# Linear attention and a token-mixing layer on one core: values copied straight into chunk order, one token order for all tensors, full-height transposes

## The chip, the cores and the metric

The kernel runs on one core of a Trainium2 chip. The core has five engines, each with its own queue of instructions that it works off in order: TensorE (matrix multiplications; PE in the profile, with PEld for its weight loads), VectorE (DVE), ScalarE (ACT), GpSimd (POOL) and SyncE (SP), which here only issues DMA transfers. Engines wait for each other by semaphores. SBUF is the working memory with 128 partitions, PSUM the small memory of 8 banks into which TensorE writes.

The metric is the time of one execution on the device in microseconds (us), lower is better. Every kernel is run several times, and the median counts.

## What is computed

The first part is a linear attention with decay. For every batch and head a 48 x 48 state is carried over 768 tokens; its output is the input of the second part, in which every batch mixes its tokens through two learned projections.

```python
# r, k, v, w: (4 batches, 8 heads, 768 tokens, 48), float32; u: (8, 48)
for t in range(S):
    cur = np.einsum('bhd,bhe->bhde', u[None] * kt, vt)
    y[:, :, t] = np.einsum('bhd,bhde->bhe', rt, state + cur)
    state = wt[:, :, :, None] * state + np.einsum('bhd,bhe->bhde', kt, vt)
x = y.transpose(0, 2, 1, 3).reshape(B, S, 384)
wq, wk = x @ w_q, x @ w_k                      # 384 x 64 each
W_tok = (1 / 8) * np.einsum('bsd,btd->bst', wq, wk)
mixed = np.einsum('bst,btd->bsd', W_tok, x)
out = np.maximum(mixed, 0.0) @ w_out           # 384 x 384
```

## The kernel before

**Tiling.** The 768 tokens of a batch are three *units* of 256 tokens, so there are 12 units (n = 0 to 11; unit n belongs to batch n // 3). A unit holds two chunks (c = 0, 1) of 128 tokens. Heads are taken in four pairs (hp). In a loaded tile a partition holds neighbouring tokens: two for `load` (128 partitions, pieces of 2 x 48 floats = 384 bytes in HBM), four for `load_long` (64 places per chunk, pieces of 768 bytes; used for k and r of all units but the first). So the tokens of a chunk stand in an order of their own, and every step that turns a tile has to put them back.

**A unit's steps**, by the names under which the plan adds them:

- `wg kg rg vg`: loads of the four tensors, on SP's queue, into rings of four buffers each. `ln` (ScalarE): logarithm of the decay. `k16`, `r16` (GpSimd or ScalarE): casts to bf16.
- `cw` (TensorE): the sum of the logarithms along the tokens, as a product with the triangular matrix CM, for each chunk with the 64 rows that hold its tokens. `en`, `ep` (ScalarE): exponentials of minus and plus that sum; `ep` is two instructions, since it also changes the order.
- `kT`, `rT` (TensorE): transposes of k and r by the permutation PM, 16 matmuls of 64 rows each. `ks`: copy of the transposed k to SBUF. `qT = r * k`, `RT = r * ep` (VectorE), `KT = k * en` (GpSimd from `ks`, or VectorE from PSUM).
- Values: `v16` (GpSimd) casts to bf16, `vp` (TensorE) permutes the tokens by PM in four matmuls, `VB` (ScalarE) copies from PSUM. For the last batch v is loaded in pieces of 192 bytes by four transfers (`vw`, `load_whole`) straight into chunk order, and `VB` is one cast on GpSimd.
- `dps`, `dd`, `Vd`: the bonus u. `A` (TensorE): the 128 x 128 scores of every head; `AM` (VectorE): their mask. `kb`, `kd`, `sn`, `SB`: the new state. `yi`, `ya`, (`yv`): the output in PSUM; `X`: its copy to SBUF, on VectorE with the bonus added.
- `xt`, `XT`, `qk`, `QK`: transposes of X and the two projections.

When a batch's three units are done: `T`, `TS` (the mixing matrix), and for each of its units `mx` (product with it), `rl` (relu), `fp` (projection by w_out, 6 matmuls of 384 columns), `os` (copy to SBUF), `st` (store). The first and the last unit are cut into halves by chunk.

**What sets the order.** All steps are added to a `Plan`. ORDER is a permutation of them, written out: every engine gets its steps in just this order, whatever unit they belong to. WAYS gives the engine of each step that has a choice (A ScalarE, D VectorE, P GpSimd; E, e and c are forms of TensorE's steps, with e and c on parts of the array; N leaves a step out, T cuts the weights' load in two). BANKS gives the PSUM bank of each buffer. `yv` is there only where `X` is on ScalarE. All matmuls go through the helper `mm`, so that they share one line of the profile, and most copies share those of `copy`.

Of the kernel before, what the change touches and what calls it, by code (L numbers as in the profile page):

```python
# [10 lines left out]
F32 = mybir.dt.float32  # L11
# [21 lines left out]
class Plan:  # L33
# [85 lines left out]
]  # L119
WAYS = (  # L120
    "PPDPPDPPDDDDDDPDTTPDDAAPPDPPPADDDEENDEAAPPDdPADEAEENDEAAAPAPPADEDcNDEDAAAAAAAAPADdPAAEAc"
    "cNDEADPPDdPAAeAcENDeDAPPDPPAAeAENDEAAAAAAAAAPPDPPAAEDEENDEAAPPDdPAAeAEENDEAAPPDPPAAEAcND"
    "EDAAADAAAAPPDPPAEAEcNDeAAPPDPPAeAccNDeDAPPDPPPAPPAENDEDADNDEAADDDDAAAAAADDADNNEEEENEEENE"
    "NENENNNNNNEN"
)
BANKS = [
# [7 lines left out]
]  # L134


WARM = 24


@with_exitstack  # L140
def kernel(
# [27 lines left out]
    LONG = tuple(range(1, N))  # L169
    WHOLE = (B - 1,)  # L170

# [13 lines left out]
    def const(shape, dtype, name):  # L185
# [9 lines left out]
        wg=(4, HW, F32), rg=(4, HW, F32), kg=(4, HW, F32), vg=(4, HW, F32), os=(4, 2 * DM, F32),  # L195
        kd=(2, KW, BF16), lw=(2, 1024, BF16), r16=(2, 1024, BF16), k16=(2, 1024, BF16),
        ep=(2, 8 * EW, BF16), en=(2, 1024, BF16), ks=(2, 1024, BF16), qT=(2, 1024, BF16),
        RT=(2, 1024, BF16), KT=(2, 1024, BF16), v16=(2, 2 * DM, BF16), VB=(2, 2 * DM, BF16),
        dd=(2, 2 * H, F32), Vd=(2, 2 * DM, BF16), AM0=(2, 1024, BF16), AM1=(2, 1024, BF16),
        SB=(4, NP * D, BF16), XT=(2, 2 * DM, BF16), MX=(4, 2 * DM, BF16), X=(2, NCH * DM, BF16),  # L200
        QK=(2, QW, BF16), TS=(2, DM, BF16), vw=(2, NCH * DM, F32))
    if not WHOLE:
        del RINGS["vw"]
# [14 lines left out]
    PM = const([C, C], BF16, "PM")  # L218
# [3 lines left out]
    CM = const([C, 2 * C], BF16, "CM")  # L222
# [7 lines left out]

    def load_long(b, i, tl, ap, e):
        nc.sync.dma_start(  # L232
            out=view(tl, 0, [[2 * D2, NP], [1, 2 * D2]]),
            in_=dataclasses.replace(ap, offset=(b * H * S + i * U) * D,
                                    ap=[[4 * D, 64], [S * D, H], [1, 4 * D]]))

    def load_whole(b, q, tl):
        nc.sync.dma_start(
            out=view(tl, 0, [[D, H * NCH], [1, D]], p0=64 * (q % 2) + 32 * (q // 2), pn=32),
            in_=dataclasses.replace(v, offset=(b * H * S + q) * D,  # L240
                                    ap=[[4 * D, 32], [C * D, H * NCH], [1, D]]))
# [54 lines left out]
    def setup():  # L296
# [11 lines left out]
        runs = [[64, 2], [32, 2], [1, 32]]  # L308
# [5 lines left out]
        clear("C", CM, 1.0, cols=128)  # L314
        for c in range(2):
            for j in range(2):
                select("C%d%d" % (c, j), ["C"], view(CM, j * C, runs, p0=c * 64, pn=64), 128,
                       ALU.is_ge, pattern=[[1, 2], [2, 2], [4, 32]], base=-j,
                       channel_multiplier=-2)
# [3 lines left out]
        clear("P", PM, cols=64)  # L323
        select("PM", ["P"], view(PM, 0, runs), 128, ALU.not_equal, 1.0,
               pattern=[[64, 2], [1, 2], [2, 32]], base=0, channel_multiplier=-1)
# [6 lines left out]
        for q in range(4):  # L332
            select("U%d" % q, ["U"], view(US, 0, runs, p0=64 * (q % 2) + 32 * (q // 2), pn=32), 128,
                   ALU.is_gt, pattern=[[1, 2], [2, 2], [4, 32]], base=-q, channel_multiplier=-4)
# [5 lines left out]
    def dma(key, fn, after=(), buf=None, reads=()):  # L340
        return add(key, "ST" if key[0] in ("wts", "wo") else "S", fn, after, buf, reads)

    def weights():
# [16 lines left out]
        def cast(e):  # L360
            nc.gpsimd.tensor_scalar_mul(view(wq_sb, 0, [[128, NK], [64, 2], [1, DH]]),
                                        view(wq_f, 0, [[DH, NK], [0, 2], [1, DH]]), scale)
            nc.gpsimd.tensor_copy(view(wk_sb, 0, [[DH, NK], [32, 2], [1, 32]]),
                                  view(wk_f, 0, [[DH, NK], [1, 2], [2, 32]]))
# [14 lines left out]
    def unit(n, batch):  # L379
# [6 lines left out]
        whole, long = b in WHOLE, n in LONG  # L386
# [3 lines left out]
        for name, ap in (("wg", w), ("kg", k), ("rg", r)) + (() if whole else (("vg", v),)):  # L390
            f = load_long if name in ("kg", "rg") and long else load
            g[name] = ring(name)
            g[name + "L"] = dma((name, n), lambda e, ap=ap, f=f, x=g[name].tile: f(b, i, x, ap, e),
                                buf=g[name])
# [204 lines left out]
        for cs in ([(0,)] if final else fine):  # L599
# [13 lines left out]
            def f_kd(e, cs=cs):  # L613
                n4 = NP * len(cs)
                x = view(at(kb, BF16), cs[0] * NP * D, [[D, n4], [1024, 2], [1, D]])
                if kb.kind == "s":
                    x = view(at(kb, BF16), 0, [[C, n4], [64, 2], [1, D]])
# [288 lines left out]
```

## Time and profile before

| | |
|---|---|
| median of 3 runs | 103.31 us |
| the runs | 101.56, 103.31, 103.33 us |
| span of the profiled execution, first to last instruction | 101.1 us |
| its own time, with what lies around the span | not given apart from the runs; 0.5 to 2.2 us over the span, by the fastest run and the median |
| granted TensorE clock | 1.00 of full speed |
| busy: TensorE / VectorE / ScalarE / GpSimd | 86.8 / 80.5 / 80.9 / 68.8 us |
| read from and written to HBM | 19.66 MB, 4.72 MB |
| DMA packets | 45165, of which 31576 under 512 bytes |

Busy time is the time in which an engine had an instruction running; neighbouring instructions overlap a little, so the durations of a group add up to more than its busy time. "Idle before" is the time in which an engine waited just ahead of an instruction, and the arrow names what ended it. A matmul's duration has a fixed part (0.16 to 0.2 us) that overlaps with its neighbours; what a step costs TensorE is read from one step's start to the next one's.

### The profile page before, as it was taken

The numbers are of one execution on the slowest core, as the hardware profiler recorded it, in microseconds if no ns is written. First come the engines' busy times: TensorE is split into PE (matmuls) and PEld (weight loads), VectorE is DVE, ScalarE is ACT, GpSimd is POOL, SyncE is SP. The second block draws the span as 40 slices with busy tenths as digits, with TensorE's granted clock in tenths as the row PEclk, the third lists the DMA queues.
The fourth block names the chain that finished last, engine by engine and source line by source line (L and its number), as shares of the span: only waits on it lengthen the run. The fifth ranks groups of instructions, "written<-read, shape, count | busy, mean of one in ns | idle before, by whom it ended". The sixth has DMA issues, their size and how long they took to land.

```text
span 101.1 us, 4474 instructions
## 1 busy us (share of the span) xinstructions
PE 86.8 (86%) x1906; PEld 63.4 (63%) x1909; DVE 80.5 (80%) x134; ACT 80.9 (80%) x134; POOL 68.8 (68%) x82
## 2 busy tenths in 40 slices
PE   5966984989899888999899988999999998999920
PEld 1334553777597556678577875787877667776500
DVE  5423896899999989889999899999997897565520
ACT  5068975999799699599998999989997995735930
POOL 6858964699937764968899749999995897000000
PEclk9999999999999999999999999999999999999999
DMA  1999998999999999999999799999888831007591
GB/s 26 309 324 346 332 317 227 341 261 274 313 306 240 257 205 244 291 329 341 224 323 287 192 343 301 166 155 250 229 233 310 314 141 67 0 0 303 209 366 69
DMA packets 45165, 24.68 MB, mean 244 GB/s; under 512 B 31576, under 2 KB 43992, under 8 KB 45144
## 3 DMA queue, kind: packets, MB, share of 16 engines
q1 hardware_dynamic: 44984, 24.19, 86.9%
q8 instruction: 15, 0.25, 1.0%
q10 hardware_dynamic: 160, 0.20, 0.6%
q14 instruction: 6, 0.05, 0.2%
HBM read 19.66 MB, written 4.72 MB: 241 GB/s over the span
## 4 chain that ended last, share of the span: by engine, by line
PE 34%; ACT 15%; DMA 13%; DVE 12%; SPq 10%; issue 7%; POOL 4%; DVEq 0%; POOLq 0%; ACTq 0%
PE PS L177 34%; DMA vg<-in_v_dram 7%; DMA kg<-in_k_dram 6%; ACT ep L444 6%; SPq L227 5%; ACT en L451 4%; SPq L232 4%; DVE AM L592 3%; DVE X L724 2%; ACT os L275 2%; POOL v L281 2%; DVE ks L281 1%; POOL r L414 1%; DVE RT L513 1%; DVE qT L503 1%
## 5 line engine op out<-in xcount | busy, mean ns | idle before, releaser
L592 DVE TENSOR_TENSOR AM<-PS,US 128x1024 bf16<-128x1024 f32 x24 | 28.7, 1216 | 0.9 <-PE PS L177 0.6
L523 POOL TENSOR_TENSOR KT<-ks,en 128x1024 bf16<-128x1024 bf16 (+1 forms) x10 | 17.4, 1739 | 2.7 <-DVE qT L503 2.0
L572 POOL TENSOR_TENSOR Vd<-VB,dd 128x768 bf16<-128x768 bf16 (+1 forms) x14 | 18.0, 1292 | 1.5 <-ACT dd L275 1.0
L444 ACT ACTIVATE ep<-PS,kp 128x512 bf16<-128x512 f32 (+1 forms) x28 | 16.3, 646 | 0.1
L451 ACT ACTIVATE en<-PS,km 128x1024 bf16<-128x1024 f32 (+1 forms) x14 | 13.9, 1002 | 1.1 <-ACT QK L275 0.8
L724 DVE TENSOR_TENSOR X<-PS,Vd 128x768 bf16<-128x768 f32 (+1 forms) x13 | 11.6, 889 | 2.7 <-POOL Vd L572 1.4
L177 PE MATMUL PS<-wo,MX 128*128 128x384 bf16 x72 | 13.3, 326 | 0.2 <-ACT ep L444 0.2
L177 PEld LDWEIGHTS <-KT 48*128 48x128 bf16 (+1 forms) x312 | 10.3, 94 | 5.1 <-issue 2.6
L177 PE MATMUL PS<-RT,KT 48*128 48x128 bf16 x192 | 9.6, 217 | 1.9 <-POOL KT L523 1.0
L414 POOL CAST k<-kg 128x768 bf16<-128x768 f32 x10 | 8.2, 824 | 3.6 <-DMA kg<-in_k_dram 1.8
L281 DVE COPY ks<-PS 128x1024 bf16<-128x1024 bf16 x11 | 7.6, 689 | 3.7 <-PE PS L177 3.7
L275 ACT COPY os<-PS 128x768 f32<-128x768 f32 (+1 forms) x13 | 8.8, 679 | 1.9 <-PE PS L177 1.6
L414 POOL CAST r<-rg 128x768 bf16<-128x768 f32 x10 | 8.2, 824 | 3.1 <-DMA rg<-in_r_dram 1.9
L513 DVE TENSOR_TENSOR RT<-PS,ep 128x1024 bf16<-128x1024 bf16 (+1 forms) x14 | 8.5, 608 | 2.2 <-ACT ep L444 2.0
L403 ACT ACTIVATE lw<-wg 128x768 bf16<-128x768 f32 x12 | 10.1, 850 | 0.1
L177 PEld LDWEIGHTS <-MX 128*128 128x128 bf16 x72 | 6.4, 97 | 4.3 <-DVE MX L289 0.3
L287 ACT ACTIVATE MX<-PS 128x768 bf16<-128x768 f32 (+1 forms) x11 | 8.2, 758 | 0.9 <-PE PS L177 0.8
L275 ACT CAST VB<-PS 128x768 bf16<-128x768 f32 x9 | 7.3, 806 | 1.8 <-PE PS L177 1.7
L281 POOL CAST v<-vg 128x768 bf16<-128x768 f32 x9 | 7.4, 823 | 1.8 <-DMA vg<-in_v_dram 1.7
L177 PE MATMUL PS<-CM,lw 64*128 64x128 bf16 x192 | 7.9, 217 | 0.7 <-issue 0.4
L656 DVE TENSOR_TENSOR SB<-PS,ep 128x192 bf16<-128x192 f32 x20 | 7.0, 350 | 1.6 <-PE PS L177 1.5
L503 DVE TENSOR_TENSOR qT<-PS,ks 128x1024 bf16<-128x1024 bf16 x12 | 8.2, 681 | 0.0
(82 smaller groups left out, 182.8 us busy)
## 6 DMA issues: line engine op xcount, KB each, us to landing
kg<-in_k_dram SPq DMA_DIRECT2D x12, 384.0 KB, 5.5
wg<-in_w_dram SPq DMA_DIRECT2D x12, 384.0 KB, 6.3
rg<-in_r_dram SPq DMA_DIRECT2D x12, 384.0 KB, 6.4
vg<-in_v_dram SPq DMA_DIRECT2D x9, 384.0 KB, 6.9
out_dram<-os SPq DMA_DIRECT2D x9, 384.0 KB, 3.2
vw<-in_v_dram SPq DMA_DIRECT2D x4, 288.0 KB
out_dram<-os SPq DMA_DIRECT2D x5, 192.0 KB, 2.8
wof<-in_moe_w_out_dram SPq DMA_DIRECT2D x1, 450.0 KB
```

The source lines that it names most:

```text
L177: return nc.tensor.matmul(o, l, rr, start=start, stop=stop, skip_group_check=True, is_transpose=trans)
L275: nc.scalar.copy(o, i)
L281: x.tensor_copy(o, i)
L403: nc.scalar.activation(view(lw.tile, 0, [[64, H], [512, 2], [1, D]]), view(g["wg"].tile, 0, [[D2, H], [D, 2], [1, D]]), ACT.Ln, bias=0.0, ...
L414: op(view(o.tile, 0, [[64, NP], [256, 4], [1, D]]), view(g[src].tile, 0, [[2 * D2, NP], [D, 4], [1, D]]))
L444: nc.scalar.activation(view(ep.tile, cs[0] * NP * EW + off, [[EW, NP * len(cs)], [step, 2], [1, 32]]), view(at(cw), cs[0] * 512 + j * 64, ...
L451: nc.scalar.activation(en.tile[:, ds(cs[0] * 512, w_)], at(cw)[:, ds(cs[0] * 512, w_)], ACT.Exp, bias=km, scale=-1.0)
L513: nc.vector.tensor_tensor(plain(RT.tile, cs, 32), turned(512, cs, True), plain(ep.tile, cs, EW // 4), ALU.mult)
L523: x.tensor_tensor(KT.tile[:, cols], ks.tile[:, cols], en.tile[:, cols], ALU.mult)
L572: (nc.vector if e == "D" else nc.gpsimd).tensor_tensor(Vd.tile[:, cols], VB.tile[:, cols], view(dd.tile, cs[0] * H, [[1, len(cs) * H], [0, ...
L592: AMs[c] = add(("AM", n, c), "D", lambda e, c=c, A=A: nc.vector.tensor_tensor(view(AM[c].tile, 0, [[C, 8], [1, C]]), view(at(A), 0, [[C, 8 ...
L724: nc.vector.tensor_tensor(o, y_, view(Vd.tile, c0 * DM, dims), ALU.add)
```

## The change

- **One token order.** All tensors are loaded by `load`, two tokens to a partition, in pieces of 384 bytes; `load_long` and `load_whole` go. Within a chunk the order is now 64 odd tokens, then 64 even ones, for r, k, v, w, the mask US and the sums; the copies `QK` and the weights' cast no longer reorder.
- **Values.** `v16`, `vp`, `VB` go. `vu` and `vs` copy from the loaded tile into VB, each as two instructions of 64 partitions x 384 elements, float32 to bf16. `vu` stays on its partitions, `vs` moves between the lower and the upper half. `vs` is on VectorE (`VSW = "D"`); `vu` has a choice.
- **Transposes and sums.** `kT` and `rT` use all 128 rows and the identity, 8 matmuls of 128 columns; they have a PSUM bank each. `cw` is 8 matmuls of 256 columns over all 128 rows, with a matrix CM of double width in which the other chunk's rows are zero. PM goes.
- **One decay exponential.** `ep` is one instruction instead of two.
- **Smaller ones.** The weights are loaded in one part each. The ring `os` has 10 buffers instead of 4.
- **ORDER, WAYS and BANKS are new throughout.** Steps by engine:

| step | before | after |
|---|---|---|
| k16, r16 | GpSimd 22, ScalarE 2 | GpSimd 21, ScalarE 3 |
| values | v16 GpSimd 9, vp TensorE 9, VB ScalarE 9 and GpSimd 3 | vu GpSimd 11 and ScalarE 1, vs VectorE 12 (two instructions each) |
| ks | ScalarE 1, VectorE 11 | ScalarE 7, VectorE 5 |
| KT | GpSimd 10, VectorE 4 | GpSimd 9, VectorE 5 |
| X | VectorE 13 | VectorE 9, ScalarE 4 (with 4 yv on TensorE) |
| XT | ScalarE 8, VectorE 5 | ScalarE 9, VectorE 4 |
| os | ScalarE 13, VectorE 2 | ScalarE 7, VectorE 8 |
| dd | ScalarE 9, VectorE 3 | ScalarE 6, VectorE 6 |
| uC (start) | ScalarE | VectorE |

On SP's queue all loads come first, then all stores; before, one store stood between the loads of units 10 and 11. The first loads are w, k, r of unit 0 (before: k, w, w of unit 1, r). On TensorE all 15 `fp` steps come after `cw` of unit 11; before, the three of batch 0 stood ahead of `cw` of unit 9. The first `KT` is on VectorE.

```diff
-    def load_long(b, i, tl, ap, e):
...
-    def load_whole(b, q, tl):
...
 def f_cw(e):
     for hp in range(NP):
         for j in range(2):
-            for c in range(2):
-                mm(x[:, ds(c * 512 + hp * C, C)],
-                   lw.tile[ds(c * 64, 64), ds(j * 512 + hp * 128, 128)],
-                   CM[ds(c * 64, 64), ds(j * C, C)],
-                   start=(hp == 0 and j == 0), stop=(j == 1))
+            mm(x[:, ds(hp * U, U)], lw.tile[:, ds(j * 512 + hp * 128, 128)],
+               CM[:, ds(j * U, U)], start=(hp % 2 == 0 and j == 0), stop=(j == 1))
...
-            def f_ep(e, cs=cs, w_=w_):
-                for off, step, j in ((68, 34, 0), (34, -33, 1)):
-                    nc.scalar.activation(
...
+            def f_ep(e, cs=cs, many=many, step_=step_):
+                nc.scalar.activation(
+                    view(ep.tile, cs[0] * EW + 1, [[step_ * EW, many], [1, C]]),
+                    view(at(cw), cs[0] * C, [[step_ * C, many], [1, C]]), ACT.Exp, bias=kp,
+                    scale=1.0)
...
+        kt, rt = bank(), bank()
+        def transposed(name, src, step, o):
+            def f(e):
+                x = at(o, BF16)
                 for hp in range(NP):
                     for j in range(2):
+                        mm(view(x, hp * U + (1 - j) * 64, [[C, 2], [1, 64]]),
+                           src.tile[:, ds(j * 512 + hp * 128, 128)], ID16, trans=True)
...
+        def f_V(moved):
+            def f(e):
+                op = dict(A=nc.scalar.copy, D=nc.vector.tensor_copy, P=nc.gpsimd.tensor_copy)[e]
+                for c in range(2):
+                    half = (c + moved) % 2
+                    op(view(VB.tile, c * DM, [[1, DM]], p0=half * 64, pn=64),
+                       view(g["vg"].tile, (1 - half) * D, [[D2, H], [1, D]], p0=c * 64, pn=64))
+            return f
+        VBs = [add(("vu", n), "PAD", f_V(0), [g["vgL"]], VB, [g["vg"]])]
+        VBs.append(add(("vs", n), VSW, f_V(1), [g["vgL"]], VB, [g["vg"]]))
```

More of the change, by code (lines that the diff above doesn't have):

```diff
@@ L167 @@
     N = B * NU
-    LONG = tuple(range(1, N))
-    WHOLE = (B - 1,)
     SHIFT = 25
@@ L331, in setup @@
         clear("U", US, 1.0, cols=64)
-        for q in range(4):
-            select("U%d" % q, ["U"], view(US, 0, runs, p0=64 * (q % 2) + 32 * (q // 2), pn=32), 128,
-                   ALU.is_gt, pattern=[[1, 2], [2, 2], [4, 32]], base=-q, channel_multiplier=-4)
+        for c in range(2):
+            select("U%d" % c, ["U"], view(US, 0, runs, p0=c * 64, pn=64), 128, ALU.is_ge,
+                   pattern=[[-c, 2], [1, 64]], base=c - 1, channel_multiplier=-1)
         su["IU"] = add(("IU",), "DP", lambda e: on(e).tensor_scalar_mul(IDU, ID16, UNIT),
@@ L340, in dma @@
     def dma(key, fn, after=(), buf=None, reads=()):
-        return add(key, "ST" if key[0] in ("wts", "wo") else "S", fn, after, buf, reads)
+        return add(key, "S", fn, after, buf, reads)
     def weights():
@@ L385, in unit @@
         fine = each if split else both
-        whole, long = b in WHOLE, n in LONG
         new = (lambda *k: [su[x + str(n)] for x in k]) if n < 2 else lambda *k: []
         g = {}
-        for name, ap in (("wg", w), ("kg", k), ("rg", r)) + (() if whole else (("vg", v),)):
-            f = load_long if name in ("kg", "rg") and long else load
+        for name, ap in (("wg", w), ("kg", k), ("rg", r), ("vg", v)):
             g[name] = ring(name)
-            g[name + "L"] = dma((name, n), lambda e, ap=ap, f=f, x=g[name].tile: f(b, i, x, ap, e),
+            g[name + "L"] = dma((name, n), lambda e, ap=ap, x=g[name].tile: load(b, i, x, ap, e),
                                 buf=g[name])
-        if whole and i == 0:
-            batch["vw"] = ring("vw")
-            batch["vwL"] = [dma(("vw", n, q), lambda e, q=q, x=batch["vw"].tile:
-                                load_whole(b, q, x), buf=batch["vw"]) for q in range(4)]
         lw = ring("lw")
@@ L428, in f_cw @@
                 for j in range(2):
-                    for c in range(2):
-                        mm(x[:, ds(c * 512 + hp * C, C)],
-                           lw.tile[ds(c * 64, 64), ds(j * 512 + hp * 128, 128)],
-                           CM[ds(c * 64, 64), ds(j * C, C)],
-                           start=(hp == 0 and j == 0), stop=(j == 1))
-        cws = add(("cw", n), "E", f_cw, [ln] + [su["C%d%d" % x] for x in ((0, 0), (0, 1), (1, 0), (1, 1))] +
-                  new("lw"), cw, [lw], mode=1)
+                    mm(x[:, ds(hp * U, U)], lw.tile[:, ds(j * 512 + hp * 128, 128)],
+                       CM[:, ds(j * U, U)], start=(hp % 2 == 0 and j == 0), stop=(j == 1))
+        cws = add(("cw", n), "E", f_cw, [ln] + [su[x] for x in ("C00", "C01", "C10", "C11", "Z0", "Z1")] +
+                  new("lw"), cw, [lw])
         en, ep = ring("en"), ring("ep")
@@ L459, in unit @@
                 eps[c], ens[c] = x, y
-        kr = wide()
-        def transposed(name, src, step, place):
+        kt, rt = bank(), bank()
+        def transposed(name, src, step, o):
             def f(e):
-                o = at(kr, BF16)
-                if long:
-                    for hp in range(2):
-                        for s in range(4):
-                            for c in range(2):
-                                rows = ds(c * 64, 64)
-                                x = c * 1024 + place + hp * C + (s % 2) * 64 + (s // 2) * 32
-                                mm(view(o, x, [[256, 2], [1, 32]]),
-                                   src.tile[rows, ds(s * 256 + hp * 128, 128)],
-                                   PM[rows, rows], trans=True)
-                    return
+                x = at(o, BF16)
@@ L476, in f @@
                 for hp in range(NP):
                     for j in range(2):
-                        for c in range(2):
-                            rows = ds(c * 64, 64)
-                            mm(o[:, ds(c * 1024 + place + hp * C + j * 64, 64)],
-                               src.tile[rows, ds(j * 512 + hp * 128, 128)],
-                               PM[rows, rows], trans=True)
-            return add((name, n), "E", f, [step, su["PM"]] + new(name[0] + "16"), kr, [src], mode=1)
-        def turned(place, cs=(0, 1), runs=False):
-            return view(at(kr, BF16), place + cs[0] * 1024, [[1024, len(cs)]] * (len(cs) > 1) +
-                        ([[32, 16], [1, 32]] if runs else [[1, 512]]))
@@ L490, in plain @@
-        def plain(t, cs=(0, 1), run=0):
-            y = 16 * (run or 32)
-            return view(t, cs[0] * y, [[y, len(cs)]] * (len(cs) > 1) +
-                        ([[run, 16], [1, 32]] if run else [[1, y]]))
-        kTs = transposed("kT", k16, k16s, 0)
-        rTs = transposed("rT", r16, r16s, 512)
+                        mm(view(x, hp * U + (1 - j) * 64, [[C, 2], [1, 64]]),
+                           src.tile[:, ds(j * 512 + hp * 128, 128)], ID16, trans=True)
+            return add((name, n), "E", f, [step, su["ID"]] + new(name[0] + "16"), o, [src])
@@ L498, in unit, with plain, slots @@
+        def plain(t, cs=(0, 1)):
+            return view(t, cs[0] * C, [[1, 1024]] if len(cs) > 1 else [[U, NP], [1, C]])
+        def slots(t, cs, w_, x, step):
+            return view(t, cs[0] * w_ + x, [[(3 - len(cs)) * w_, NP * len(cs)], [step, 2], [1, 64]])
+        kTs = transposed("kT", k16, k16s, kt)
+        rTs = transposed("rT", r16, r16s, rt)
         ks = ring("ks")
-        kss = add(("ks", n), "AD", lambda e: copy(e, plain(ks.tile), turned(0)), [kTs], ks, [kr],
+        kss = add(("ks", n), "AD", lambda e: copy(e, ks.tile, at(kt, BF16)), [kTs], ks, [kt],
@@ L527, in unit @@
                     cols=512 * len(cs), half=half,
-                    more=dict(P=([kss], [ks]), D=([kss], [ks]), d=([kTs], [kr])))
+                    more=dict(P=([kss], [ks]), D=([kss], [ks]), d=([kTs], [kt])))
             for c in cs:
@@ L532, in unit @@
         VB = ring("VB")
[L533 to L554 removed]
+        def f_V(moved):
+            def f(e):
+                op = dict(A=nc.scalar.copy, D=nc.vector.tensor_copy, P=nc.gpsimd.tensor_copy)[e]
+                for c in range(2):
+                    half = (c + moved) % 2
[4 more added lines that the diff above has]
+        VBs.append(add(("vs", n), VSW, f_V(1), [g["vgL"]], VB, [g["vg"]]))
         dps, dd = bank(), ring("dd")
@@ L593, in unit @@
                 view(AM[c].tile, 0, [[C, 8], [1, C]]), view(at(A), 0, [[C, 8], [1, C]]),
-                view(US, 0, [[0, 8], [1, C]]), ALU.mult), [As] + [su["U%d" % q] for q in range(4)],
+                view(US, 0, [[0, 8], [1, C]]), ALU.mult), [As] + [su["U0"], su["U1"]],
                 AM[c], [A])
-        kb, kd = either() if len(fine) == 1 else wide(), ring("kd")
+        kb, kd = either() if len(fine) == 1 else bank(), ring("kd")
         kds = {}
@@ L600, in f_kb @@
             def f_kb(e, cs=cs):
-                for cp in range(NP * cs[0], NP * (cs[-1] + 1)):
-                    if e == "E":
-                        mm(at(kb, BF16)[:, ds(cp * C, C)], KT.tile[:, ds(cp * C, C)], ID16,
-                           trans=True)
-                        continue
-                    for hh in range(2):
-                        mm(at(kb, BF16)[:, ds(hh * 1024 + cp * D, D)],
-                           KT.tile[ds(hh * 64, D), ds(cp * C, C)],
-                           ID16[ds(hh * 64, D), ds(hh * 64, D)], trans=True)
-            x = add(("kb", n, cs[0]), "eE" if kb.kind == "x" else "e", f_kb,
+                for c in cs:
+                    for hp in range(NP):
+                        cp = c * NP + hp
+                        x = ds((2 * hp + c) * C, C)
+                        if e == "E":
+                            mm(at(kb, BF16)[:, ds(cp * C, C)], KT.tile[:, x], ID16, trans=True)
+                            continue
+                        for hh in range(2):
+                            mm(at(kb, BF16)[:, ds(hh * 1024 + cp * D, D)],
+                               KT.tile[ds(hh * 64, D), x],
+                               ID16[ds(hh * 64, D), ds(hh * 64, D)], trans=True)
+            x = add(("kb", n, cs[0]), "eE" if kb.kind == "x" else "E", f_kb,
                     [KTs[c] for c in cs], kb, [KT], cols=len(cs), mode=dict(e=1, E=0))
```

140 lines of the change are left out of this document (47 added, 93 removed), and 83 rows, old and new, of tables (BANKS, ORDER).

## The prediction

> **What bounds the kernel now.** I read the page first, then the busy time in stretches cut where the pace changes, then the order of time on TensorE.
>
> ```profile
> span 101.1 us, 4474 instructions
> ...
> PE 34%; ACT 15%; DMA 13%; DVE 12%; SPq 10%; issue 7%; POOL 4%; DVEq 0%; POOLq 0%; ACTq 0%
> ...
> core 0: us, PE busy (x) PEld busy (x) DVE busy (x) ACT busy (x) POOL busy (x), PEclk, DMA share, GB/s
> 6.60:60.20 53.60, 47.10 (x1188) 35.95 (x1192) 47.59 (x76) 48.29 (x77) 40.40 (x40) 1.00 1.05 286
> 60.20:85.20 25.00, 23.88 (x594) 18.65 (x595) 23.17 (x33) 22.82 (x41) 22.41 (x21) 1.00 0.88 224
> 85.20:96.80 11.60, 11.36 (x123) 7.38 (x116) 6.68 (x13) 7.86 (x16) 0.72 (x1) 1.00 0.36 136
> ```
>
> The second line is the chain that ended last, by engine: TensorE leads with a third, and no engine has half. The stretches say why. Up to 60 us TensorE, VectorE and ScalarE are each busy 88 to 90% and the DMA engines are full: nobody has much room, nobody is alone the limit. From 60.2 to 96.8 us TensorE is busy 35.24 of 36.6 us, and behind 85 us it is the only one that is full. So a microsecond of TensorE work behind 60 us costs nearly a microsecond, and before that only what the others don't cover. The clock is 1.00 throughout.
>
> The profiled execution has a span of 101.1 us. The three times are 101.56, 103.31 and 103.33, so 0.5 to 2.2 us lie around the span; I make the sum as a difference and put it on the median, 103.3.
>
> **The change part by part: TensorE.** All its work has one source line, so I go by time, from one step's first start to the next one's.
>
> ```profile
> 47.17 0.40 PE L177 MATMUL PS<-RT,KT 48*128 48x128 bf16 x8
> 47.39 0.65 PE L177 MATMUL PS<-CM,lw 64*128 64x128 bf16 x16
> ...
> 60.16 0.62 PE L177 MATMUL PS<-CM,lw 64*128 64x128 bf16 x16
> 60.61 0.39 PE L177 MATMUL PS<-RT,KT 48*128 48x128 bf16 x8
> 60.94 0.35 PE L177 MATMUL PS<-wk,XT 128*128 128x64 bf16 x6
> ...
> 63.15 0.36 PE L177 MATMUL PS<-v,PM 64*64 64x384 bf16 x4 [0.34 <-ACT ep L444]
> 63.51 0.50 PE L177 MATMUL PS<-ID,X 128*128 128x128 bf16 x6
> 63.94 0.41 PE L177 MATMUL PS<-PM,k 64*128 64x64 bf16 x16
> 64.18 0.40 PE L177 MATMUL PS<-PM,r 64*128 64x64 bf16 x16
> 64.41 0.28 PE L177 MATMUL PS<-SB,RT 48*128 48x48 bf16 x8
> ...
> 70.93 0.83 PE L177 MATMUL PS<-ID,X 128*128 128x128 bf16 x12
> 71.69 0.62 PE L177 MATMUL PS<-RT,KT 48*128 48x128 bf16 x16
> ...
> 72.76 0.49 PE L177 MATMUL PS<-XT,wq 128*128 128x256 bf16 x3
> 73.09 0.61 PE L177 MATMUL PS<-ID,KT 128*128 128x128 bf16 x8
> ...
> 93.69 3.10 PE L177 MATMUL PS<-wo,MX 128*128 128x384 bf16 x18
> ```
>
> The decay sum cw takes 0.45 us (60.16 to 60.61): 16 matmuls of 128 columns, 28 ns each, because the halves of 64 rows run beside each other. It becomes 8 matmuls of 256 columns over all rows, half of whose matrix is zero. Three matmuls of 256 columns took 0.33 us (72.76 to 73.09), so eight take 0.88: **+0.43 per unit**. A transpose step takes 0.24 us (63.94 to 64.18) and becomes 8 full transposes; twelve such took 0.76 us (70.93 to 71.69), so eight take 0.5: **+0.26 each, two per unit**. Fewer instructions, but more time. Against it: vp goes, 0.36 us in nine of the units (63.15 to 63.51). And fewer changes between half-array and full-array steps: the score step A took 0.22 us ahead of another half-array step (47.17 to 47.39) and 0.33 ahead of a full one (60.61 to 60.94), so 0.11 us for a change to full rows; the other directions I bound by 0 and 0.11.
>
> What counts is TensorE behind 60 us, which is where cw of unit 9 stands. From that step on I count the two orders. Three cw: +1.3. Transposes, six before and five after: 5 x 0.5 - 6 x 0.24 = +1.1. One vp: -0.4. Two score steps fewer: -0.7. One mixing step mx (three matmuls of 256 columns) more: +0.3. The output projections fp of batch 0 are moved here, 15 instead of 12; eighteen of their matmuls took 3.10 us, six about 1.0: +3.0. Array changes 37 to 22: 5 of them to full rows, -0.55 to -1.65, I take -1.0. The other steps nearly cancel. Sum +3.6. TensorE's idle time there is 1.36 us, so +2.2 to +3.6, and I take **+2.9**. The early part takes the moved 3.0 us off, and gets 9 x 0.43 + 19 x 0.5 - 18 x 0.24, less eight vp (2.9) and 24 changes (about 1.9), plus two score steps and four yv (about 2): +3 net against 6.5 us of idle TensorE (53.6 less 47.10), which I cost at nothing. If that cover is gone, it is +3 more.
>
> **VectorE, ScalarE, GpSimd.** Rows grouped by line and shape:
>
> ```profile
> L281 DVE COPY XT<-PS 128x384 bf16<-128x384 bf16 x1 | 0.3, 348 | 0.0
> L281 DVE COPY os<-PS 128x384 f32<-128x384 f32 x1 | 0.6, 556 | 1.9 <-ACT os L275 1.9
> L335 DVE TENSOR_SCALAR IDU<-ID 128x128 bf16<-128x128 bf16 x1 | 0.2, 195 | 0.7 <-POOL ID L301 0.7
> L724 DVE TENSOR_TENSOR X<-PS,Vd 128x768 bf16<-128x768 f32 x11 | 10.5, 950 | 1.6 <-POOL Vd L572 1.4
> L281 DVE COPY ks<-PS 128x1024 bf16<-128x1024 bf16 x11 | 7.6, 689 | 3.7 <-PE PS L177 3.7
> ...
> L444 ACT ACTIVATE ep<-PS,kp 128x512 bf16<-128x512 f32 x20 | 12.9, 709 | 0.0
> L451 ACT ACTIVATE en<-PS,km 128x1024 bf16<-128x1024 f32 x10 | 11.3, 1126 | 0.8 <-ACT QK L275 0.8
> L275 ACT CAST VB<-PS 128x768 bf16<-128x768 f32 x9 | 7.3, 806 | 1.8 <-PE PS L177 1.7
> ...
> L572 POOL TENSOR_TENSOR Vd<-VB,dd 128x768 bf16<-128x768 bf16 x10 | 14.7, 1476 | 0.4 <-ACT dd L275 0.3
> L523 POOL TENSOR_TENSOR KT<-ks,en 128x1024 bf16<-128x1024 bf16 x6 | 12.8, 2128 | 2.3 <-DVE qT L503 2.0 <-DVE X L724 0.2
> L281 POOL CAST v<-vg 128x768 bf16<-128x768 f32 x9 | 7.4, 823 | 1.8 <-DMA vg<-in_v_dram 1.7
> ```
>
> VectorE gets 24 copies vs of 64 x 384, float32 in SBUF to bf16, which no row shows. Above: 556 ns (same length, float32, from PSUM). Below: 195 ns, the one SBUF to SBUF row, with a third of the elements. Between lies 348 ns (bf16, from PSUM); I take 350, the middle. Up to the last mask it loses five X (4.7 us by the row), six ks (4.1) and two XT, and gains two os and some small steps: about -7 with the overlap of neighbours. So the copies break even at 7 / 24 = 0.29 us, and at 0.35 VectorE has 1.4 us more in the 7.8 us that it idles from 6.6 to 85.2. I cost it at nothing; by 556 ns it is +6.3, of which little fits.
>
> ScalarE loses nine VB (7.3 us), the second instruction of ep (1.42 to 1.13 per unit, 3 us in all), and six os to VectorE; it gains six ks, four X and a few casts: level within 2 us. GpSimd trades 12 value casts of 0.82 us for 22 half ones (I take 0.5) and loses one KT: level, and it isn't the bound.
>
> A new wait: vs stands in VectorE's own order and waits for its load. Behind vs of unit 1 queue SB and AM of units 0 and 1, and TensorE for them. That load is the tenth issued in both orders, and RT and qT ahead of it run in the meantime: nothing to 1.3 us; I take nothing.
>
> **Start and loads.**
>
> ```profile
> 5.96 0.30 ACT L275 CAST uC<-uR 8x128 bf16<-8x128 f32 x1 [3.90 <-DMA uR<-in_u_dram]
> 6.17 1.57 ACT L403 ACTIVATE lw<-wg 128x768 bf16<-128x768 f32 x2
> 9.46 0.42 DVE L513 TENSOR_TENSOR RT<-PS,ep 128x512 bf16<-128x512 bf16 x1 [1.70 <-ACT ep L444]
> ...
> 3.00:6.00 3.00, 2.68 (x7) 0.68 (x5) 0.59 (x4) 0.04 (x1) 2.57 (x8) 1.00 1.17 325
> 34.00:39.00 5.00, 4.16 (x109) 2.86 (x106) 4.72 (x7) 4.17 (x7) 2.45 (x4) 1.00 1.12 209
> 63.00:67.00 4.00, 3.85 (x108) 3.03 (x109) 3.86 (x6) 3.68 (x8) 4.00 (x5) 1.00 1.12 147
> ...
> POOL v L281 <- DMA vg<-in_v_dram: 1.7, 2, 1.3
> POOL k L414 <- DMA kg<-in_k_dram: 1.3, 1, 1.3
> ```
>
> The first logarithm stands behind uC, which waits for a small load. uC goes to VectorE and the decay load is issued first: about 1 us earlier, and RT waits for just that chain. The wider cw takes 0.4 of it back; the first KT moves off GpSimd. **-1.0** (-0.4 to -1.4).
>
> Pieces of 384 bytes, the only kind in flight from 3 to 6 us, moved 325 GB/s. The dips, 209 GB/s with the weights in two parts and 147 with the values of batch 3 in 192-byte pieces, go: 1.8 and 2.2 us of transfer at 325 GB/s. The change loses the 768-byte pieces of k and r, which can't be worth more. All stores go behind all loads on SP's queue, where there is room after 70 us. Who waited for loads is GpSimd, some 3 us in all behind 10 us: **-1.0** (0 to -2). The Trainium skill, "DMA: Bandwidth & Descriptors", Specifications, asks for 512 bytes or more for full rate; were 384 bytes half rate, the loads alone would outlast the kernel. The 325 GB/s decide against it here.
>
> Sum: -1.0 - 1.0 + 2.9 = +0.9: **104.2 us**.
>
> **Rivals.** *Faster: the waits, not the work, set the time.* Values reach VB without GpSimd, TensorE and ScalarE in turn, two PSUM banks per unit come free, and no load waits behind a store. For it: VectorE idles 6.0 us from 6.6 to 60.2, waiting for TensorE, ScalarE and GpSimd in turn. If 4 to 5 us of that close, the late stretch begins as much earlier: 104.2 - 4.5 = 99.7. Against it: each of those waits is short, and the late stretch has more to do.
>
> *Slower: the copies vs hold up VectorE.* Its place is the 24 copies, the price what one takes from start to start; from 0.29 us it costs, and the idle 7.8 us are gone at 0.6 us. If a copy has to let a running GpSimd instruction end first, it waits for half of one: GpSimd is busy 75% up to 60 us with instructions of 0.5 to 2.1 us, weighted by their length half of one is some 0.6 us, so 0.45 us on average and 11 us in all. With the 1.4 above, less the idle 7.8, it is +4.4: 108.6. For it: GpSimd has few gaps. Against it: its casts all took 0.82 us, so nothing disturbed it, but VectorE ran no SBUF copy beside it. The Trainium skill, "SBUF — State Buffer", Who interferes with whom, says that such a copy in a two-port mode and a GpSimd instruction shut each other out wholly; no run here shows it yet.
>
> *The change doesn't do what it says:* order, engines and banks are all new, so the gain or loss may be the order's, as the 3.0 us of moved projections are. That lies within the forecast's range.
>
> **How the numbers follow.** Forecast 0.42: 104.2, its own range 102 to 106.5 from the ends above. Faster 0.33, 97.5 to 101.2. Slower by vs 0.25, 105.5 to 112. The range 98.8 to 109.5 leaves out a third of each rival, under 0.2. Two per cent, 2.1 us, is about what a measurement of this kernel can tell from no change: 101.2 to 105.4. Faster 0.34, same 0.29 (0.7 of the forecast), slower 0.37 (the rest and vs).
>
> **What would show it.** cw near 0.9 us and each transpose step near 0.5 us from start to start; TensorE full from some 60 us on, with four or five more projections there; vs at 350 ns with no idle time ahead; uC gone from ScalarE and the first RT near 8.5 us; a load rate of 325 GB/s without dips. Wrong if vs shows long durations or GpSimd's casts leave 0.82 us, or if TensorE gets its full stretch from 55 us on.

## The result, and the profile after

The changed kernel takes **107.87 us** (median of 107.79, 108.9, 107.04 and 107.94), the kernel before 103.0 (101.56, 103.31, 103.33 and 102.68): a ratio of 1.056, with a 95% interval of 1.048 to 1.064. The change costs 5 to 6 us, by the medians or by the ratio. The profiled execution took 107.79 us, 1.7 of them around its span. Some executions take over 1.5% longer than the fastest one of their kernel, often at a lower granted clock; the ratios, here and below, leave these out, the medians take all.

The page of the changed kernel first: its span, busy times by engine, the chain that ended last, and the groups of the copies `vs` (VectorE) and `vu` (GpSimd).

```profile
span 106.1 us, 3860 instructions
...
PE 90.4 (85%) x1599; PEld 69.9 (66%) x1599; DVE 90.7 (86%) x156; ACT 80.1 (76%) x117; POOL 69.5 (66%) x89
...
GB/s 42 318 325 325 324 321 283 248 320 187 232 310 201 255 290 300 316 286 273 307 306 302 265 283 347 322 197 0 6 0 0 6 0 331 218 335 180 258 320 147
...
PE 30%; DVE 19%; issue 5%; POOL 1%; POOLq 1%; DVEq 0%
...
L483 DVE CAST VB<-vg 64x384 bf16<-64x384 f32 x24 | 13.9, 579 | 0.7
...
L483 POOL CAST VB<-vg 64x384 bf16<-64x384 f32 x22 | 11.4, 516 | 1.7 <-DMA vg<-in_v_dram 1.1
```

VectorE was busy for 80.5 us before and is for 90.7 now, and its share of the chain went from 12 to 19%. The 24 copies make up 13.9 us of it. The same stretches as in the prediction, and one more up to the last matmul (start and end, length, then busy time of TensorE, weight loads, VectorE, ScalarE and GpSimd, granted clock, DMA share, GB/s):

```profile
6.60:60.20 53.60, 46.18 (x922) 38.27 (x922) 51.44 (x86) 46.21 (x63) 43.47 (x49) 1.00 1.06 283
60.20:85.20 25.00, 22.39 (x440) 18.07 (x438) 24.48 (x39) 20.54 (x31) 18.38 (x19) 1.00 0.47 132
85.20:96.80 11.60, 11.23 (x191) 8.37 (x189) 8.56 (x16) 7.39 (x12) 2.27 (x2) 1.00 0.55 215
96.80:102.30 5.50, 5.28 (x36) 3.07 (x35) 3.76 (x8) 3.51 (x9) 0.00 (x0) 1.00 0.69 264
```

VectorE is now busy 51.44 of 53.6 us and 24.48 of 25: from 7 to 85 us it is by far the fullest engine, which none was before. That it sets the pace there is tested below. TensorE idles 7.4 us in the first stretch (6.5 before) and waits. Whom it waits for stands in brackets in its order of time:

```profile
55.00 1.03 PE L175 MATMUL PS<-CM,lw 128*128 128x256 bf16 x8
55.87 0.61 PE L175 MATMUL PS<-ID,k 128*128 128x128 bf16 x8
56.32 0.56 PE L175 MATMUL PS<-VB,AM 128*128 128x48 bf16 x16
...
61.01 1.03 PE L175 MATMUL PS<-CM,lw 128*128 128x256 bf16 x8
...
67.57 0.38 PE L175 MATMUL PS<-RT,KT 48*128 48x128 bf16 x7 [1.47 <-DVE RT L461]
...
99.13 3.09 PE L175 MATMUL PS<-wo,MX 128*128 128x384 bf16 x18
```

That RT came late because it stands behind copies in VectorE's order. Two of the twelve pairs, with what stands around them:

```profile
42.12 0.74 DVE L483 CAST VB<-vg 64x384 bf16<-64x384 f32 x2
42.78 0.35 DVE L266 TENSOR_SCALAR kd<-PS 128x384 bf16<-128x384 bf16 x1
...
63.99 2.21 DVE L483 CAST VB<-vg 64x384 bf16<-64x384 f32 x2
66.22 0.69 DVE L452 TENSOR_TENSOR qT<-PS,ks 128x1024 bf16<-128x1024 bf16 x1
66.83 0.69 DVE L461 TENSOR_TENSOR RT<-PS,ep 128x1024 bf16<-128x1024 bf16 x1
```

And GpSimd at the same times:

```profile
40.56 1.07 POOL L483 CAST VB<-vg 64x384 bf16<-64x384 f32 x2
43.03 1.48 POOL L505 TENSOR_TENSOR Vd<-VB,dd 128x768 bf16<-128x768 bf16 x1 [1.39 <-DVE VB L483]
...
63.27 2.13 POOL L466 TENSOR_TENSOR KT<-ks,en 128x1024 bf16<-128x1024 bf16 x1 [0.68 <-ACT dd L258]
65.35 1.22 POOL L483 CAST VB<-vg 64x384 bf16<-64x384 f32 x2
```

At 42.12 GpSimd idles (41.63 to 43.03), and the pair takes 0.74 us. At 63.99 GpSimd is 0.7 us into a KT that ends at 65.40, and the pair takes 2.21. The single durations, by source line in that window (smallest, median, largest), are the first copy's 1.63 us, until 0.2 us behind the end of KT, and 0.56:

```profile
L483 DVE CAST VB<-vg x2: 564/1096/1627, 64.0 to 65.6; 64x384 bf16<-64x384 f32 x2
```

All four pairs that meet an idle GpSimd (at 17.05, 42.12, 78.53 and 86.19) have copies of 0.353 to 0.356 us, 0.72 to 0.74 a pair; the other eight take 0.95 to 2.21. Loads ran at 284 and 331 GB/s beside the first two of them (16.5 to 18 and 42 to 43 us), so it isn't the transfers that stretch a copy. So a copy takes 0.354 us, and 13.9 - 24 x 0.354 = **5.4 us is waiting for GpSimd**. This is the rule of the Trainium skill, "SBUF — State Buffer", Who interferes with whom: a VectorE copy in a two-port mode and a GpSimd instruction shut each other out, and who starts first keeps the ports to its end. The trace agrees with the shutting out; in which mode a copy ran no view shows. It was nearly one-sided here, as GpSimd's casts show, the kernel before first:

```profile
L414 POOL CAST k<-kg 128x768 bf16<-128x768 f32 x10 | 8.2, 824 | 3.6 <-DMA kg<-in_k_dram 1.8
L389 POOL CAST k<-kg 128x768 bf16<-128x768 f32 x10 | 8.2, 830 | 2.5 <-DMA kg<-in_k_dram 2.4
```

The start came out as forecast: `uC` is on VectorE, and the first RT starts at 8.55 us, 9.46 before. VectorE's order of time:

```profile
5.56 0.21 DVE L264 CAST uC<-uR 8x128 bf16<-8x128 f32 x1 [2.82 <-DMA uR<-in_u_dram]
...
8.55 0.70 DVE L461 TENSOR_TENSOR RT<-PS,ep 128x512 bf16<-128x512 bf16 x2
```

### The profile page after: what moved, and what is told of

Its sections match the earlier page's. It is cut to its first block, busy times and chain, and to the rows that moved or that the text cites. A ratio compares the mean times of both kernels' runs of the same rounds, so it can differ in the third digit from the quotient of the medians.

```text
span 106.1 us, 3860 instructions
## 1 busy us (share of the span) xinstructions
PE 90.4 (85%) x1599; PEld 69.9 (66%) x1599; DVE 90.7 (86%) x156; ACT 80.1 (76%) x117; POOL 69.5 (66%) x89
## 2 busy tenths in 40 slices
DMA packets 53313, 24.62 MB, mean 232 GB/s; under 512 B 50992, under 2 KB 52144, under 8 KB 53296
## 4 chain that ended last, share of the span: by engine, by line
PE 30%; DVE 19%; issue 5%; POOL 1%; POOLq 1%; DVEq 0%
PE PS L175 30%; DVE AM L525 5%; DVE VB L483 4%; DVE X L660 4%; DVE os L264 1%; POOL Vd L505 1%; DVE qT L452 1%; DVE RT L461 1%; DVE SB L592 1%; POOLq L834 1%; DVE ks L264 0%; DVE kd L266 0%; DVE dd L264 0%; DVEq L264 0%; DVEq L660 0%
## 5 line engine op out<-in xcount | busy, mean ns | idle before, releaser
L483 DVE CAST VB<-vg 64x384 bf16<-64x384 f32 x24 | 13.9, 579 | 0.7
L175 PE MATMUL PS<-CM,lw 128*128 128x256 bf16 x96 | 12.5, 273 | 1.4 <-ACT lw L379 1.1
L413 ACT ACTIVATE ep<-PS,kp 128x1024 bf16<-128x1024 f32 (+1 forms) x14 | 13.7, 1002 | 0.0
L483 POOL CAST VB<-vg 64x384 bf16<-64x384 f32 x22 | 11.4, 516 | 1.7 <-DMA vg<-in_v_dram 1.1
L175 PEld LDWEIGHTS <-lw 128*128 128x128 bf16 x96 | 8.6, 97 | 3.9 <-ACT lw L379 2.3
L389 POOL CAST r<-rg 128x768 bf16<-128x768 f32 x11 | 9.3, 842 | 0.6 <-DMA rg<-in_r_dram 0.5
L258 ACT COPY XT<-PS 128x768 bf16<-128x768 bf16 x9 | 7.2, 802 | 2.6 <-PE PS L175 2.6
L660 DVE TENSOR_TENSOR X<-PS,Vd 128x768 bf16<-128x768 f32 (+1 forms) x9 | 7.7, 863 | 1.4 <-POOL Vd L505 0.7
L175 PE MATMUL PS<-ID,k 128*128 128x128 bf16 x96 | 7.3, 219 | 1.4 <-POOL k L389 0.8
L175 PE MATMUL PS<-VB,AM 128*128 128x48 bf16 x192 | 7.7, 184 | 0.8 <-DVE AM L525 0.8
```

Of the source, the lines that this page charges most:

```text
L175: return nc.tensor.matmul(o, l, rr, start=start, stop=stop, skip_group_check=True, is_transpose=trans)
L389: op(view(o.tile, 0, [[64, H], [512, 2], [1, D]]), view(g[src].tile, 0, [[D2, H], [D, 2], [1, D]]))
L413: nc.scalar.activation(view(ep.tile, cs[0] * EW + 1, [[step_ * EW, many], [1, C]]), view(at(cw), cs[0] * C, [[step_ * C, many], [1, C]]), ...
L483: op(view(VB.tile, c * DM, [[1, DM]], p0=half * 64, pn=64), view(g["vg"].tile, (1 - half) * D, [[D2, H], [1, D]], p0=c * 64, pn=64))
L660: nc.vector.tensor_tensor(o, y_, view(Vd.tile, c0 * DM, dims), ALU.add)
```

## The experiments

Two theories. *Port:* VectorE sets the pace, and the waiting of the copies is what was lost. *TensorE:* the added and deferred TensorE work is, whoever copies.

| kernel | median, us | kernel before on the same chip | ratio (95%) |
|---|---|---|---|
| vs on ScalarE | 111.12 | 103.38 | 1.080 (1.071 to 1.088) |
| vs a fill of 0.206 us | 102.15 | 103.38 | 0.989 (0.983 to 0.995) |
| vs nearly gone | 102.55 | 103.38 | 0.989 (0.976 to 1.002) |
| cw on half arrays | 108.37 | 103.38 | 1.040 (1.026 to 1.053) |
| vs a fill of 0.353 us | 103.62 | 102.87 | 1.008 (1.002 to 1.013) |
| before + 24 copies | 129.63 | 102.87 | 1.265 (1.255 to 1.275) |
| before + 24 fills | 111.75 | 102.87 | 1.091 (1.078 to 1.103) |
| vs on GpSimd | 109.37 | 102.87 | none; its four runs range from 106.5 to 110.51 us |
| before, late projections | 110.35 | 103.76 | 1.079 (1.065 to 1.093) |
| vs mixed | 106.26 | 103.76 | 1.042 (1.034 to 1.050) |
| vs mixed, cw on half arrays | 107.41 | 103.76 | 1.052 (1.042 to 1.062) |
| before, new start | 102.52 | 102.82 | 0.992 (0.986 to 0.997) |

**Fills in place of the copies.** Three kernels, the same order throughout:

```diff
-VBs.append(add(("vs", n), VSW, f_V(1), [g["vgL"]], VB, [g["vg"]]))
+def f_ms(e, w_=354 if n > 1 else DM):        # second kernel: 2; third: 353
+    for c in range(2):
+        nc.vector.memset(view(VB.tile, c * DM, [[1, w_]], p0=(c + 1) % 2 * 64, pn=64), 0.0)
+VBs.append(add(("vs", n), VSW, f_ms, [g["vgL"]], VB, [g["vg"]]))
```

> In place of each copy vs a fill with zeros by VectorE of the same 64 partitions of VB, 354 columns (384 in the first two units), by the rows of the other fills about 0.35 us, the same as an undisturbed copy; half of the values are left out. It reads no SBUF. Theory 'port': all 24 take 0.35 to 0.38 us, 5.4 us of waiting is gone from VectorE, and the time falls by 3 to 5 us, to 103 to 105. Rival 'length': it is the added VectorE instructions as such that cost, and rival 'TensorE': 107 to 108.5, no change.

> As the fill, but only 2 columns from unit 2 on (the first two units fill 384), so that nearly all VectorE time of vs goes; half of the values are left out. Theory 'port': a further 20 x 0.29 = 6 us of VectorE go; TensorE becomes the bound and the time is 1 to 4 us below the fill, 100 to 103. Rival 'length': all of the gain comes here and none with the fill, 101 to 104 against 107 to 108. Rival 'TensorE': still 106 to 108.

> The first fill took 0.206 us, less than the 0.354 of an undisturbed copy (its row: 64x177 uint32), so it took away length as well as waiting. Here the fill has 353 columns, an odd number, in bf16 (384 in the first two units); by the row of the bf16 fills of 128 and 256 columns (0.165 and 0.272 us) it takes 0.35 us. Half of the values are left out. Theory 'port': waiting alone costs, and the time is that of the first fill, 101.5 to 103.5. Rival 'length': the 3.5 us of length that the first fill saved count, 104.5 to 107.

The first fill took 0.206 us, not 0.35, and gave 0.989. With next to no work in its place it is still 0.989, where 1 to 4 us less had been expected. The fill of 353 columns has the length of an undisturbed copy in 20 of 24 places; the four of the first two units, with 384 columns, take 0.218 us. Its group, and its stretches:

```profile
L490 DVE MEMSET VB<- 64x353 bf16 x20 | 7.1, 353 | 2.6
```

```profile
6.60:60.20 53.60, 47.54 (x937) 39.66 (x935) 48.40 (x88) 46.34 (x65) 43.68 (x49) 0.98 1.02 269
60.20:85.20 25.00, 24.28 (x465) 19.03 (x462) 22.31 (x37) 21.13 (x32) 17.81 (x18) 0.96 0.59 164
```

Nothing stretches it, VectorE has 5.2 and 2.7 us idle again, and the kernel is nearly level with before: 1.008 against 1.056. TensorE is busy 24.28 of 25 us behind 60 us, here under a clock of 0.96; with the fills of 0.206 us it is busy 24.62 of the same 25 us under a clock of 1.00.

The 4.8 points between the copies and these fills, 4.9 us, go with the 5.4 us of waiting. The length itself isn't free: it costs the 1.9 points, about 2 us, between this fill and the other two. So the median of 103.62 us lies between the ranges of the two theories, 0.1 us above that of 'port'. As accounts of the whole loss 'length' and 'TensorE' fall.

A fill differs from a copy in two more ways. It doesn't wait for the load of v; in the changed kernel VectorE idled only 0.7 us ahead of the copies. And it doesn't hold the loaded tile, so that later loads could come sooner. They didn't: ScalarE waits 5.5 us for the loads of w with these fills, 3.3 with the copies.

**The same work added to the kernel before**, where nothing waits for its results:

```diff
+XS = const([C, HW], F32, "XS")
+XD = const([C, 768], BF16, "XD")
...
+if s["key"][0] == "AM" and s["key"][2] == 0:
+    for x in range(2):
+        nc.vector.tensor_copy(view(XD, x * DM, [[1, DM]], p0=64, pn=64),
+                              view(XS, x * D, [[D2, H], [1, D]], pn=64))
+        # other kernel: nc.vector.memset(view(XD, x * DM, [[1, 353]], p0=64, pn=64), 0.0)
```

> The kernel before, with two copies of 64x384 float32 to bf16 from SBUF to SBUF added on VectorE behind the first mask AM of each unit, 24 in all; nothing waits for what they write. Theory 'port': they wait for GpSimd, which is as busy as in the changed kernel, and take 0.5 to 0.65 us each, 13 to 15 us in all against 7.8 us of idle VectorE: 107 to 110. Rival 'length': 24 x 0.354 = 8.5 us, as the fill of the same length: both alike within 1 us, wherever they lie.

> The same with 24 fills of 353 columns (0.35 us) on VectorE in place of the copies. Theory 'port': 8.5 us on 7.8 us of idle VectorE, most of it covered: 103 to 105.5, at least 3 us below the copies. Rival 'length': the same as the copies.

Groups of the kernel with copies:

```profile
L883 DVE CAST XD<-XS 64x384 bf16<-64x384 f32 x24 | 18.9, 826 | 0.4
...
L416 POOL CAST r<-rg 128x768 bf16<-128x768 f32 x10 | 8.8, 876 | 0.0
```

And of the one with fills:

```profile
L883 DVE MEMSET XD<- 64x353 bf16 x24 | 8.5, 353 | 1.9
```

The copies wait 0.47 us each, the fills not at all; here GpSimd loses too (its r casts 0.876 us, 0.824 before). Which of the two is dearer was as expected; both sizes were missed. The fills' 8.5 us cost 8.9, under a lower clock than before (0.94 from 6.6 to 60.2 us, 1.00 before), so no cover by the idle 7.8 us of VectorE shows at that place, right behind the first mask. The copies cost 17.9 us more than the fills, for 11.3 us more in their durations. Part of the rest may be the clock's: from 6.6 to 60.2 us it was 0.75 with the copies and 0.94 with the fills. The two stretches, copies first:

```profile
6.60:60.20 53.60, 42.76 (x851) 30.86 (x850) 44.20 (x65) 36.61 (x58) 32.95 (x33) 0.75 1.02 284
```

```profile
6.60:60.20 53.60, 45.08 (x1055) 33.44 (x1055) 46.76 (x80) 44.34 (x70) 39.17 (x39) 0.94 1.04 286
```

How much of the 17.9 us is the clock's and how much the chain's was not separated.

**The copies on another engine.**

```diff
-VSW = "D"
+VSW = "A"      # other kernels: "P", with KT of units 3, 4, 6 on VectorE; "ADADDDAPAPDD", one letter a unit
```

> The changed kernel with all 24 copies vs on ScalarE instead of VectorE, nothing else. Theory 'port': the copies wait on VectorE for running GpSimd instructions (13.9 us for 24 copies that take 0.354 each undisturbed, so 5.4 us of waiting), and VectorE, busy 96 to 98% from 7 to 88 us, sets the pace. Then VectorE loses 13.9 us, ScalarE gains 24 copies of about 0.45 us, 11 us, on top of the 66.8 it is busy of the 78.6 us from 6.6 to 85.2; so ScalarE comes near its own limit, and the time falls to 103.5 to 106. No copy on ScalarE shows a wait for GpSimd. Rival 'TensorE': the later TensorE work (3.7 us more behind 60 us) is all of the loss, whoever copies: 107 to 109.

> The changed kernel with all 24 copies vs on GpSimd, and in exchange KT of units 3, 4 and 6 on VectorE from PSUM (0.69 us each instead of 2.13 on GpSimd); the order is kept. Theory 'port': VectorE loses 13.9 us and gains 2.1, none of its instructions can wait for GpSimd any more, and GpSimd gains 12.4 - 6.4 = 6 us on 62 of 78.6: 101.5 to 104, near the fill. Rival 'TensorE': 107 to 108.5. If GpSimd becomes the bound, its idle time is gone and TensorE waits for KT and for VB: 105 or more.

> The changed kernel with vs of units 0, 2, 6 and 8 on ScalarE and of units 7 and 9 on GpSimd; the other six stay on VectorE, four of which ran at 0.36 us a copy. The result is the whole reference. Theory 'port': VectorE loses 9.1 us by the rows of those pairs (1.30, 1.39, 1.59, 1.37, 2.21, 1.25), most of the waiting among them, ScalarE gains 4.2 and GpSimd 2.1: 103 to 105. If other copies now meet GpSimd instructions instead, or ScalarE holds up TensorE as it did with all copies: 106 to 108.

On ScalarE no copy is stretched (0.51 us each, 26 with two of vu), but ScalarE is then busy 50.58 of 53.6 us and 24.25 of 25:

```profile
6.60:60.20 53.60, 45.95 (x897) 38.17 (x897) 41.86 (x68) 50.58 (x76) 40.84 (x48) 0.97 1.06 282
60.20:85.20 25.00, 21.73 (x413) 17.57 (x413) 20.73 (x31) 24.25 (x38) 18.74 (x19) 1.00 0.49 136
```

It is slower than the changed kernel, a miss: I had named ScalarE's limit and not priced it. On GpSimd (106.5 to 110.51 us) GpSimd is busy 24.01 of 25 us from 60.2, and all four runs lie above 105 us: the condition "if GpSimd becomes the bound" came true. Whether it is slower or faster than the changed kernel these runs don't tell. Mixed, 1.4 points, 1.5 us, are won, with intervals that just touch, where the theory had 3 to 5; the second range, 106 to 108, came true. The twelve copies left on VectorE still take 0.487 us, and ScalarE, busy 48.69 of 53.6, has eight more. No engine has 8 to 12 us to give, so none of the three moves comes back to the kernel before.

**cw on half arrays**, 16 matmuls of 64 rows as before, once in the changed kernel and once in the mixed one:

```diff
-        mm(x[:, ds(hp * U, U)], lw.tile[:, ds(j * 512 + hp * 128, 128)],
-           CM[:, ds(j * U, U)], start=(hp % 2 == 0 and j == 0), stop=(j == 1))
+        for c in range(2):
+            mm(x[:, ds(c * 512 + hp * C, C)],
+               lw.tile[ds(c * 64, 64), ds(j * 512 + hp * 128, 128)],
+               CM[ds(c * 64, 64), ds((2 * j + c) * C, C)],
+               start=(hp == 0 and j == 0), stop=(j == 1))
```

> The changed kernel with the decay sum cw as before, 16 matmuls of 128 columns on 64 rows each instead of 8 of 256 columns on all rows; the exponentials read the two banks in three dimensions. TensorE does 12 x 0.43 = 5.2 us less, 1.3 of it behind 60 us. Rival 'TensorE': the time falls by 1.3 us and by part of the rest, to 104 to 106.5. Theory 'port': TensorE idles 7.4 us before 60 us anyway and waits for VectorE, so only a part of the late 1.3 counts: 106.5 to 107.9.

> The same with cw on half arrays, 16 matmuls of 64 rows, in the form of the kernel before: 5.2 us less TensorE work in all, 1.3 of it behind 60 us. If VectorE's waits are gone and TensorE sets the pace behind 60 us, 1.3 to 3 us below the mixed kernel: 100.5 to 103, at or below the kernel before. If VectorE still sets it: within 1 us of the mixed kernel.

It takes 5.2 us off TensorE by the prediction's rows, and the ratio goes from 1.056 to 1.040 in the one and from 1.042 to 1.052 in the other. The intervals overlap, the signs differ, and both medians lie above what was expected: no gain is shown. The second profile says why the comparison is blunt: there the clock stood at 0.50 for 6.8 us.

**The deferral alone**, in the kernel before:

```diff
# ORDER: fp and os of units 0, 1, 2 from ahead of cw of unit 9 to behind cw of unit 11; BANKS to suit
-os=(4, 2 * DM, F32)
-MX=(4, 2 * DM, BF16)
+os=(7, 2 * DM, F32)
+MX=(7, 2 * DM, BF16)
```

> The kernel before, with only the three output projections of batch 0 and their copies os (ScalarE, as before) moved behind cw of unit 11, and their stores behind the store of unit 5; the rings MX and os get 7 buffers for it. It does the deferral alone. By the prediction's term it puts 3.0 us of TensorE work into the stretch behind 60 us, which has 1.36 us of idle TensorE, and takes it out of a stretch with 6.5 us of idle: plus 1.6 to 3.0 us, 104.5 to 106. Rival: the early part ends as much earlier, so nothing is lost: 102 to 104.

It costs 7.9%, some 8 us, where 1.6 to 3.0 were expected. In the profiled execution, of 112.03 us, cw of unit 9 starts at 63.72 us (60.16 before), so 3.6 us are lost where work had only been taken away, under a clock of 0.87:

```profile
6.60:60.20 53.60, 46.41 (x1078) 34.72 (x1079) 44.24 (x71) 43.15 (x68) 39.74 (x39) 0.87 1.06 289
```

The projections seem to have filled pauses of TensorE there; that was argued from the clock, not tried. In the changed kernel, whose order differs throughout, the same deferral seems to cost less, since with the copies nearly gone it runs at 0.989; it was not tried there by itself.

**The start alone**, in the kernel before:

```diff
# ORDER: loads begin with w, k, r of unit 0, then w of unit 1; uC on VectorE, ahead of ks of unit 0
```

> The kernel before with the start of the change alone: the loads begin with w, k and r of unit 0, then w of unit 1, and uC is on VectorE ahead of ks of unit 0 instead of on ScalarE ahead of the first logarithm. The prediction's term says 1.0 us (0.4 to 1.4) earlier at the first RT, and as much at the end, since nothing behind it waits for loads at that time: 101.5 to 102.6. If another wait takes its place at the start (PM or the first cast of r on GpSimd, which come no earlier), or if the gain is lost before 60 us, where no engine alone is full: 102.6 to 103.5, no change.

With 0.8% less (0.3 to 1.4) it is the only version with the whole computation that is ahead of the kernel before, and by less than the 2% that the prediction took to be measurable. But not by the reason given: in its profile the first RT starts at 10.48 us, a microsecond later than before. The second logarithm stands ahead of the first exponential, as before, and now waits 2.81 us for its load, which has become the fourth instead of the third; in the changed kernel it stands behind the exponentials of unit 0, and this order was not taken over. So the run doesn't test the term of the start. The last mask starts at 84.66 instead of 85.42; where that comes from is open.

## Why the prediction was right and wrong, point by point

The range held 107.9, and its rival *Slower: the copies vs hold up VectorE* (108.6) is what happened; the forecast of 104.2 is not.

- **The step that failed:** "I cost it at nothing", of the 24 copies. Their length was right (0.350 forecast, 0.354 measured), but it isn't free: about 2 us by the ratios 1.008 and 0.989. What was missing above all is the waiting, 4.9 us. With next to nothing in the copies' place, all the rest of the change came out at 0.989, some 1 us faster than before, where the sum had +0.9. So with fills of the copies' length the kernel is at +0.8 us, next to the forecast, but by luck: two misses of about 2 us cancel.
- **The rival's size** came out right by two errors. It priced the wait at 0.45 us a copy, 11 us; it was 5.4 us, 0.22 a copy, since at least a third of the copies met an idle GpSimd. And it took 7.8 us of idle VectorE off as cover; 4.9 of the 5.4 us were lost. Placed behind the first mask, a copy waited 0.47 us and no cover showed.
- **Early part, start and loads:** cw of unit 9 was to start 2 us sooner and starts at 61.01, 0.85 later. Of the waiting, 3.4 us lies ahead of it (eight pairs, 9.3 us, against 0.73 a pair); with fills of 0.206 us it starts at 58.67, 1.5 sooner than before. The first RT was forecast near 8.5 and is at 8.55. The loads dip to 187 GB/s (the page's row of 40 slices), so "325 without dips" is wrong.
- **Late TensorE:** counted from cw of unit 9 on, as the prediction counts, TensorE is busy 38.10 us, 35.27 before: +2.8, against the sum of +3.6. The +3 net of the early part doesn't show at all (46.99 us from 6.6 us to that step, 47.06 before). Single steps were sized well: cw 0.87 (0.88 forecast), a transpose step 0.45 (0.5). What failed is "TensorE full from some 60 us on": it idles 3.1 us there instead of 1.36, and from cw of unit 9 to the last matmul's end pass 41.2 us instead of 36.6, +4.6 against +2.9. The 2.0 us of waiting in the last four pairs is about as much as the added idle time, and with fills of 0.206 us TensorE idles only 0.7 us of the 38.5 between the same two points. That a TensorE microsecond behind 60 us counts fully is not shown: half-array cw gave no gain.
- **"vs at 350 ns with no idle ahead"** was the right place to look, and "GpSimd's casts leave 0.82 us" the weaker sign: they moved by 0.01 to 0.02 us, while VectorE's copies took 0.579 us on average and up to 1.63.

## What to carry to other kernels

Before a copy from SBUF to SBUF is put on VectorE, count how long GpSimd's instructions beside it are: here a copy was sure of its own length only where GpSimd idled. Don't count on idle time summed over a stretch to cover work with a fixed place in an engine's order; here 8.5 us of fills that nothing waits for cost 8.9, under a clock of 0.94. And price the wait, as the rival did, place by place, before costing an edit at nothing.

## What the runs showed of the hardware

In these runs the granted clock sometimes halves behind a pause of TensorE of little more than a microsecond, and sometimes doesn't. Ahead of cw of unit 1 TensorE idles 1.10 us in both kernels below. With cw on half arrays (pause, then what follows) the clock goes to 0.50 for 3.42 us:

```profile
10.94:12.04 1.10, 0.00 (x1) 0.00 (x1) 1.04 (x3) 1.10 (x3) 0.89 (x2) 1.00 1.17 325
12.18:15.60 3.42, 3.42 (x54) 2.86 (x51) 2.98 (x6) 3.42 (x5) 1.78 (x3) 0.50 1.17 324
```

In the changed kernel, behind the same pause, it stays at 1.00:

```profile
11.02:12.12 1.10, 0.00 (x1) 0.00 (x1) 1.04 (x3) 1.10 (x3) 0.88 (x2) 1.00 1.17 325
12.18:15.60 3.42, 2.99 (x49) 2.38 (x49) 2.97 (x6) 3.42 (x5) 1.78 (x3) 1.00 1.17 323
```

In the mixed kernel with half-array cw, around the end of a pause of 1.47 us, the clock stood at 0.50 for twice that length, 6.84 us. What makes the difference these runs don't show. The Trainium skill, "TensorE: Matmul & The Clock Gate", Part 1, has a free-running window of 3.4 us, which the length agrees with; it also puts the halved clock behind a whole idle window, and that is not what these runs show, with pauses of 1.10 and 1.47 us.
